# The order of work items in a segment, written anew for each of four places

## The chip, the cores and the metric

One core of a Trainium2 chip runs the whole kernel as one program. The metric is the device time of one execution in microseconds (us), here the median of three runs.

## The reference

Two branches are computed from the same input `x` (2048 tokens, width 640) and mixed by a gate:

```
g = sigmoid((x * gate_w).sum(-1))
b = (gelu(x @ w_gate) * (x @ w_up)) @ w_down
mem = mem0                                   # 8 rows
for s in range(64):                          # segments of 32 tokens
    h = concat(mem, x[32*s : 32*s+32])       # 40 rows
    q, k, v = h @ Wq, h @ Wk, h @ Wv         # 32 heads of 192
    p = softmax(mask(q @ k.T * 192**-0.5))
    o = (p @ v) @ Wo
    mem, a[s] = o[:8], o[8:]
out = g * a + (1 - g) * b
```

The recurrence is in `mem`: the first eight output rows of a segment are rows of the next segment's input. So the 64 segments run one after the other.

## The kernel before

The program first computes branch `b` and parks it in device memory. Then `segment(s)` runs 64 times. A segment at place `q = s % 4` works through a list of items, `PROGS[q]`. The list sets the order in which all engines' instructions are recorded; each engine then runs its own instructions in that order and waits on semaphores where it needs another engine's result.

The 32 heads are taken in four octets. Even segments go through the octets upward, odd ones downward. The items:

- `("g", n, k)`: step k of 5 of the projections of group n (`proj`). `GROUPS` says which: group 0 is Q and K of the first octet, group 1 V of the first and Q, K of the second, group 2 V of the second and Q, K of the third, group 3 V of the third and Q of the last, group 4 K of the last, group 5 V of the last. One projection step is four matmuls of 384 columns side by side (lines 1138 and 226), here called a quad. At place 0, V for the left-over rows is a further quad in groups 2, 3 and 5. After the fifth step ScalarE evacuates each result (line 1159 for Q and K, 1162 for V).
- `("tq", i)`, `("tk", i)`: VectorE transposes the rows of Q or K (line 1176). They issue nothing on TensorE.
- `("sc", i)`: the mask and the scores of octet i on TensorE (lines 1187 to 1202, 234), then maximum and subtraction on VectorE (1214, 1216).
- `("ex", i)`: the exponent on ScalarE (1226), sum, reciprocal and products on VectorE (1228 to 1233).
- `("pt", i)`: p transposed on TensorE (1249, 1254), evacuated by ScalarE (1267), for the last octet in part by VectorE.
- `("pv", i)`: p times V on TensorE (1282, 1284), evacuated by ScalarE (1310, 1320) and for the last octet also by VectorE (1314).
- `("wo", i, h)`: half of octet i's output projection (line 1338, for the last octet 1364, at place 3 line 1383).
- `("lf", u, x, k)`, `("le", ...)`: Q and K of the tokens that a later segment will need beside its memory rows ("left" work: line 930 and 226, evacuated by 1411 and 1413). Only items whose first number equals the place are run there. `("vb", k)` is V of that kind at place 3.

At a segment's end VectorE adds the halves of the output (1350, 1580), transposes the memory rows into the next segment's input (1583), and the next segment's group 0 starts.

The weights do not all fit on the chip. Thirteen pieces of Q, K and V and three of Wo are swapped in every segment: as soon as a piece of the first octet has been used, `swap_loads` has SyncE's queue load the piece of the last octet into its place (line 635). That one is used at the end of this segment and the beginning of the next. The queue of SyncE runs in the order of the list, too. Which pieces are resident follows from the order of the "g" and "wo" items in `seg_order`.

Before the change, places 0 and 2 share one list, `PROG`; place 1 has it with `("ex", 3)` moved just ahead of `("pv", 2)`; place 3 has its own, `PROG3`.

Of the kernel before, what the change touches and what calls it, by code (L numbers as in the profile page):

```python
# [238 lines left out]
def _build(nc, A_x, A_mem0, A_Wq, A_Wk, A_Wv, A_Wo, seg_len, w_gate, w_up, w_down,  # L239
# [282 lines left out]
    def piece_view(key, o):  # L522
        if key[0] == 3:
# [1 line left out]
        return bview(o, GQ)  # L525

    GROUPS = [[(0, 0), (1, 0)], [(2, 0), (0, 1), (1, 1)], [(2, 1), (0, 2), (1, 2)], [(2, 2), (0, 3)], [(1, 3)], [(2, 3)]]
    PROG = [("g", 0, 0), ("g", 0, 1), ("g", 0, 2), ("g", 0, 3), ("g", 0, 4), ("tq", 0), ("g", 1, 0), ("g", 1, 1),
# [12 lines left out]
    PROG3 = [("g", 0, 0), ("g", 0, 1), ("g", 0, 2), ("g", 0, 3), ("g", 0, 4), ("tq", 0), ("g", 1, 0), ("tk", 0),  # L541
# [8 lines left out]
    PROG1 = [item for item in PROG if item != ("ex", 3)]  # L550
    PROG1.insert(PROG1.index(("pv", 2)), ("ex", 3))
    PROGS = (PROG, PROG1, PROG, PROG3)
    assert NOCT == 4
    WOP = 4
    NWP = NT
# [14 lines left out]
    def seg_order(s):  # L570
        keys = []
        for item in PROGS[s % 4]:
            if item[0] == "g":
# [817 lines left out]
    mids, n_wos, to_store = set(), [], []  # L1391
    for x, prog in enumerate(PROGS):
        at = prog.index
# [5 lines left out]
        for u in range(2):  # L1399
# [6 lines left out]
            else:  # L1406
                assert at(("le", x, u, 0)) > max(at(("wo", 3, 1)), at(("pv", 3)))
    nqkvs = [[i for i, item in enumerate(prog) if item[0] == "g"][-1] for prog in PROGS]

# [36 lines left out]

    assert all(prog.index(("wo", NOCT - 2, 1)) < prog.index(("pv", NOCT - 1)) for prog in PROGS[:3])
    assert all(prog.index(("sc", NOCT - 1)) < prog.index(("pv", NOCT - 2)) and ("g", 3, EK) in prog[:prog.index(("sc", NOCT - 1))] for prog in PROGS)
    ek_at = [prog.index(("pv", NOCT - 2)) for prog in PROGS]

# [176 lines left out]
def bass_gated_mix__memory_aug_recurrent_mem_tr__glu_gated_geglu__prompt_kernel(  # L1627
    nc,
    A_x,
    A_mem0,  # L1630
    A_Wq,
    A_Wk,
    A_Wv,
    A_Wo,
    A_seg_len,
    B_x,
    B_w_gate,
    B_w_up,
    B_w_down,
    gate_w,  # L1640
    out,
):
    _build(nc, A_x, A_mem0, A_Wq, A_Wk, A_Wv, A_Wo, A_seg_len, B_w_gate, B_w_up, B_w_down, gate_w, out)
# [33 lines left out]
```

## Time and profile before

| | before |
|---|---|
| runs | 1657.43, 1655.54, 1647.93 us, median 1655.54 us |
| profiled execution, span | 2114.2 us (no other time is listed for it) |
| granted clock in the profiled execution | 0.654 |
| TensorE busy | 2098.0 us, 99% |
| VectorE, ScalarE, GpSimd busy | 48%, 38%, 26% |
| DMA | 499.28 MB, mean 236 GB/s over the span |

The profiled execution is one execution, and it took 459 us longer than the median of the timed runs. Shares of busy time are shares of its span. A matmul's end is modelled, so a busy TensorE need not be at its peak. TensorE's weight loads are listed as an engine of their own, PEld. In a row of a group, the numbers after the bar are the busy time in us, the mean of one in ns, and the engine's idle time just before, with what ended it. In a timeline row the first number is the start and the second the length, in us.

### The profile page before, as it was taken

Reading aid. Unit: us, or ns where it says so; the run is one execution under the profiler, and the core shown is the slowest. Engines: PE = TensorE matmul, PEld = TensorE weight load, DVE = VectorE, ACT = ScalarE, POOL = GpSimd, SP = SyncE. Lnnn points to the kernel's source line nnn. Section 1 sums busy time; section 2 is a strip of 40 time slices with the busy share of each in tenths; the row PEclk is TensorE's granted clock in tenths of the full one; section 3 lists DMA queues with packets and bytes.
Section 4 is the critical chain, followed back from the end, with each engine's and each line's share of the span. In section 5 each row is a group of like instructions: output and inputs, shape, how many; then the busy total and the mean of one; then the engine's idle time right before and its main releaser. Section 6 shows DMA issues by size and latency. Waiting matters only on the chain.

```text
span 2114.2 us, 75845 instructions
## 1 busy us (share of the span) xinstructions
PE 2098.0 (99%) x37107; PEld 958.1 (45%) x28147; DVE 1005.8 (48%) x3039; ACT 792.9 (38%) x1890; POOL 553.3 (26%) x1625
## 2 busy tenths in 40 slices
PE   9999999999999999999999999999999999999997
PEld 3444344444444444444444444444444444444444
DVE  4233254554545454545545454545455454545453
ACT  1111244343434343444434343434444343434342
POOL 1000023232232223232222323232322223222332
PEclk6666666666666666666666666666666666666666
DMA  9612577776768777677767677776777676777775
GB/s 319 182 33 57 184 268 260 248 270 232 253 219 275 244 258 241 227 255 254 274 233 249 221 268 249 255 251 225 248 256 270 239 258 212 261 256 249 254 264 174
DMA packets 275415, 499.28 MB, mean 236 GB/s; under 512 B 121119, under 2 KB 136327, under 8 KB 275079
## 3 DMA queue, kind: packets, MB, share of 16 engines
q1 hardware_dynamic: 271000, 491.30, 68.8%
q8 instruction: 255, 4.18, 0.8%
q10 hardware_dynamic: 4079, 3.14, 0.5%
q14 instruction: 81, 0.66, 0.1%
HBM read 473.25 MB, written 21.09 MB: 234 GB/s over the span
## 4 chain that ended last, share of the span: by engine, by line
PE 99%; DMA 0%; DVE 0%; SPq 0%; POOL 0%; ACT 0%; issue 0%; ACTq 0%; POOLq 0%; DVEq 0%
PE ps L226 26%; PE ps L1138 25%; PE ps L1338 9%; PE ps L1383 8%; PE ps L1282 4%; PE ps L930 4%; PE ps L839 4%; PE ps L836 4%; PE ps L862 3%; PE ps L1364 3%; PE ps L1187 2%; PE ps L1284 2%; PE ps L234 1%; PE ps L1195 1%; PE ps L971 1%; PE ps L1254 1%
## 5 line engine op out<-in xcount | busy, mean ns | idle before, releaser
L226 PE MATMUL ps<-arena 128*32 128x384 bf16 x8960 | 887.8, 430 | 0.4 <-ACT arena L1159 0.4
L1138 PE MATMUL ps<-arena 128*32 128x384 bf16 x8640 | 857.5, 420 | 2.0 <-DVE arena L1583 2.0
L1138 PEld LDWEIGHTS ps<-arena 128*32 128x32 bf16 x8640 | 303.3, 117 | 525.3 <-issue 379.7
L1176 DVE STREAM_TRANSPOSE arena<-arena 128x384 bf16<-128x384 bf16 x512 | 276.5, 562 | 144.1 <-ACT arena L1159 144.1
L1159 ACT ACTIVATE arena<-ps 128x384 bf16<-128x384 f32 x512 | 230.0, 491 | 160.1 <-PE ps L1138 160.1
L1214 DVE TENSOR_REDUCE arena<-ps 104x4 f32<-104x160 f32 x256 | 83.0, 324 | 340.2 <-PE ps L1202 340.2
L1338 PE MATMUL ps<-arena 128*32 128x320 bf16 x3456 | 241.0, 404 | 0.0
L1012 POOL COPY arena<-arena 128x96 bf16<-128x96 bf16 x256 | 70.2, 274 | 475.3 <-PE ps L1202 311.4
L1267 ACT ACTIVATE arena<-ps 128x448 bf16<-128x448 f32 x192 | 104.4, 544 | 237.7 <-PE ps L1254 233.3
L1179 POOL COPY arena<-arena 64x160 bf16<-64x160 bf16 x256 | 81.9, 320 | 385.5 <-DVE arena L1176 384.3
L1162 ACT ACTIVATE arena<-ps 128x384 bf16<-128x384 f32 x256 | 125.2, 489 | 128.1 <-PE ps L1138 127.5
L1383 PE MATMUL ps<-arena 128*64 128x320 bf16 x1536 | 169.6, 387 | 0.0
L1226 ACT ACTIVATE ps<-ps 104x160 f32<-104x160 f32 x256 | 74.8, 292 | 239.5 <-DVE ps L1216 239.5
L1320 ACT ACTIVATE arena<-ps 128x480 bf16<-128x480 f32 x192 | 109.5, 570 | 93.8 <-PE ps L1284 85.7
L930 PE MATMUL ps<-arena 128*32 128x384 bf16 x1280 | 142.5, 408 | 0.0
L1338 PEld LDWEIGHTS ps<-arena 128*32 128x32 bf16 x3456 | 113.3, 129 | 56.9 <-ACT arena L1261 18.1
L1282 PE MATMUL ps<-arena 128*64 128x160 bf16 x1536 | 135.2, 263 | 0.0
L1284 PE MATMUL ps<-arena 128*64 128x64 bf16 x1536 | 128.6, 225 | 0.0
L1228 DVE TENSOR_REDUCE arena<-ps 104x4 f32<-104x160 f32 x256 | 81.8, 319 | 88.4 <-ACT ps L1226 87.4
L1383 PEld LDWEIGHTS ps<-arena 128*64 128x64 bf16 x1536 | 93.2, 127 | 49.4 <-issue 9.6
L1282 PEld LDWEIGHTS ps<-arena 128*64 128x64 bf16 x1536 | 94.1, 126 | 42.8 <-ACT arena L1159 23.0
L1411 ACT ACTIVATE arena<-ps 128x384 bf16<-128x384 f32 x120 | 57.3, 491 | 123.9 <-DVE arena L1580 74.0
(102 smaller groups left out, 2518.2 us busy)
## 6 DMA issues: line engine op xcount, KB each, us to landing
arena<-in_A_Wk_dram SPq DMA_DIRECT2D x335, 384.0 KB, 5.8
arena<-in_A_Wv_dram SPq DMA_DIRECT2D x335, 384.0 KB, 8.4
arena<-in_A_Wo_dram SPq DMA_DIRECT2D x205, 480.0 KB, 4.3
arena<-in_A_Wq_dram SPq DMA_DIRECT2D x209, 384.0 KB, 4.8
arena<-left_qk_scratch SPq DMA_DIRECT2D x126, 96.0 KB, 3.9
left_qk_scratch<-arena SPq DMA_DIRECT2D x49, 192.0 KB, 4.6
left_qk_scratch<-arena SPq DMA_DIRECT2D x30, 96.0 KB, 3.7
ffn_b_scratch<-arena ACTq DMA_DIRECT2D x16, 160.0 KB, 2.3
```

The costliest lines, as they stand in the source:

```text
L226: return e.add_instruction(mybir.InstMatmult(name=nm, start_tensor_calc=like["start"], stop_tensor_calc=stop, tile_size=(128, 32), tile_po ...
L930: fns.append(lambda e, outp=outp, rhs=rhs, j=j: e.matmul(outp, lhs, rhs, start=(k == 0), stop=(k == KT - 1), tile_position=(0, 32 * j)))
L1138: fns.append(lambda e, outp=outp, rhs=rhs, j=j: e.matmul(outp, lhs, rhs, start=(k == 0), stop=(k == KT - 1), tile_position=(0, 32 * j)))
L1159: S_.add("act", lambda e, m=m, bk=bk: e.activation(out=rows_sb[m], in_=ps[:, bk, 0:384], func=ACTF.Copy), reads=[r_ps[bk]], writes=[r_rows ...
L1162: S_.add("act", lambda e, i=i, bk=bk: e.activation(out=v_sb[i % NVB].rearrange("p (c n) -> p c n", c=3), in_=ps[:, bk, 0:384].rearrange("p ...
L1176: S_.add("dve", lambda e: e.transpose(out=dst[:, :, 0:L], in_=rows_sb[m].rearrange("p (c r) -> p c r", r=L)), reads=[r_rows[m]], writes=[r ...
L1267: S_.add("act", lambda e: e.activation(out=PT, in_=ps[:, bank, 0:PTW + 128], func=ACTF.Copy), reads=[r_ps[bank]], writes=[r_PT], name="pT ...
L1282: return [lambda e: e.matmul(full, v[:, e0:e0 + 64], PTm[:, i], start=True, stop=False, tile_position=(0, 64 * i), skip_group_check=True), ...
L1284: lambda e: e.matmul(part, vl[:, e0:e0 + 64], PTl[:, i], start=False, stop=True, tile_position=(0, 64 * i), skip_group_check=True)]
L1320: S_.add("act", lambda e: e.activation(out=apx(u[:, 0, 0, :], [[rs, na], [3 * rs, 4], [1, R]]), in_=ps[:, A, 0:na * W].rearrange("p (c t r ...
L1338: fns.append(lambda e, i=i, t=t, j=j, gv=gv: e.matmul(ps[32 * j:32 * j + 32, bank, 0:2 * DJ].rearrange("p (h n) -> p h n", h=2), lhs2[i], ...
L1383: S_.add("pe", [lambda e, i=i, g_=g_, c=c, p=p, u=u: e.matmul(ps[64 * i:64 * i + 64, LB, 0:2 * DJ], u[:, c, :], g_[:, c, 2 * DJ * i:2 * DJ ...
```

## The change

The lists of items are replaced. Each place has its own list now, with the items that run there alone; the left-over items of other places, which were skipped, no longer stand in it. Each place's list holds the same items as before, in another order. In the words of its author, all work items of a segment were searched anew for each of the four places separately, with a replay that uses the durations of the trace. `GROUPS` and all functions stay as they are.

```diff
--- before.py
+++ after.py
@@ -525,31 +525,45 @@
         return bview(o, GQ)
 
     GROUPS = [[(0, 0), (1, 0)], [(2, 0), (0, 1), (1, 1)], [(2, 1), (0, 2), (1, 2)], [(2, 2), (0, 3)], [(1, 3)], [(2, 3)]]
-    PROG = [("g", 0, 0), ("g", 0, 1), ("g", 0, 2), ("g", 0, 3), ("g", 0, 4), ("tq", 0), ("g", 1, 0), ("g", 1, 1),
-            ("tk", 0), ("g", 1, 2), ("sc", 0), ("g", 1, 3), ("ex", 0), ("g", 1, 4), ("g", 2, 0), ("g", 2, 1),
-            ("g", 2, 2), ("lf", 1, 0, 0), ("pt", 0), ("tq", 1), ("tk", 1), ("sc", 1), ("g", 2, 3), ("g", 2, 4),
-            ("tq", 2), ("ex", 1), ("lf", 2, 1, 0), ("lf", 1, 0, 1), ("lf", 1, 0, 2), ("pv", 0), ("g", 3, 0),
-            ("tk", 2), ("g", 3, 1), ("g", 3, 2), ("g", 3, 3), ("pt", 1), ("lf", 2, 1, 1), ("g", 3, 4), ("sc", 2),
-            ("ex", 2), ("pv", 1), ("wo", 0, 0), ("g", 4, 0), ("g", 4, 1), ("lf", 0, 1, 0), ("g", 4, 2),
-            ("lf", 1, 0, 3), ("lf", 1, 0, 4), ("lf", 1, 1, 0), ("lf", 1, 1, 1), ("le", 1, 0, 0), ("tq", 3),
-            ("g", 4, 3), ("le", 1, 0, 1), ("g", 4, 4), ("g", 5, 0), ("g", 5, 1), ("pt", 2), ("wo", 0, 1), ("tk", 3),
-            ("sc", 3), ("pv", 2), ("g", 5, 2), ("wo", 1, 0), ("ex", 3), ("g", 5, 3), ("wo", 1, 1), ("g", 5, 4),
-            ("wo", 2, 0), ("pt", 3), ("wo", 2, 1), ("pv", 3), ("lf", 1, 1, 2), ("lf", 2, 1, 2), ("lf", 0, 1, 1),
-            ("lf", 0, 1, 2), ("wo", 3, 0), ("wo", 3, 1), ("lf", 2, 1, 3), ("lf", 2, 1, 4), ("le", 2, 1, 0),
-            ("le", 2, 1, 1), ("lf", 1, 1, 3), ("lf", 1, 1, 4), ("le", 1, 1, 0), ("le", 1, 1, 1), ("lf", 0, 1, 3),
-            ("lf", 0, 1, 4), ("le", 0, 1, 0), ("le", 0, 1, 1)]
+    PROG0 = [("g", 0, 0), ("g", 0, 1), ("g", 0, 2), ("g", 0, 3), ("g", 0, 4), ("tq", 0), ("g", 1, 0), ("g", 1, 1),
+             ("g", 1, 2), ("g", 1, 3), ("tk", 0), ("g", 1, 4), ("sc", 0), ("g", 2, 0), ("g", 2, 1), ("tq", 1),
+             ("ex", 0), ("tk", 1), ("g", 2, 2), ("g", 2, 3), ("g", 2, 4), ("pt", 0), ("sc", 1), ("tk", 2),
+             ("tq", 2), ("ex", 1), ("g", 3, 0), ("g", 3, 1), ("g", 3, 2), ("pv", 0), ("g", 3, 3), ("g", 3, 4),
+             ("pt", 1), ("sc", 2), ("g", 4, 0), ("g", 4, 1), ("tq", 3), ("g", 4, 2), ("g", 4, 3), ("ex", 2),
+             ("g", 4, 4), ("tk", 3), ("pv", 1), ("g", 5, 0), ("wo", 0, 0), ("g", 5, 1), ("pt", 2), ("wo", 0, 1),
+             ("sc", 3), ("ex", 3), ("pv", 2), ("wo", 1, 0), ("g", 5, 2), ("g", 5, 3), ("wo", 1, 1), ("g", 5, 4),
+             ("wo", 2, 0), ("pt", 3), ("lf", 0, 1, 0), ("wo", 2, 1), ("pv", 3), ("lf", 0, 1, 1), ("lf", 0, 1, 2),
+             ("wo", 3, 0), ("wo", 3, 1), ("lf", 0, 1, 3), ("lf", 0, 1, 4), ("le", 0, 1, 0), ("le", 0, 1, 1)]
+    PROG1 = [("g", 0, 0), ("g", 0, 1), ("g", 0, 2), ("g", 0, 3), ("g", 0, 4), ("tq", 0), ("tk", 0), ("g", 1, 0),
+             ("g", 1, 1), ("g", 1, 2), ("sc", 0), ("g", 1, 3), ("ex", 0), ("g", 1, 4), ("g", 2, 0), ("g", 2, 1),
+             ("g", 2, 2), ("pt", 0), ("tq", 1), ("g", 2, 3), ("tk", 1), ("g", 2, 4), ("sc", 1), ("pv", 0),
+             ("tq", 2), ("g", 3, 0), ("g", 3, 1), ("lf", 1, 0, 0), ("g", 3, 2), ("ex", 1), ("g", 3, 3),
+             ("lf", 1, 0, 1), ("g", 3, 4), ("tk", 2), ("lf", 1, 0, 2), ("pt", 1), ("sc", 2), ("tq", 3), ("ex", 2),
+             ("g", 4, 0), ("g", 4, 1), ("lf", 1, 0, 3), ("pv", 1), ("g", 4, 2), ("lf", 1, 0, 4), ("le", 1, 0, 0),
+             ("le", 1, 0, 1), ("g", 4, 3), ("g", 4, 4), ("g", 5, 0), ("wo", 0, 0), ("pt", 2), ("lf", 1, 1, 0),
+             ("wo", 0, 1), ("lf", 1, 1, 1), ("g", 5, 1), ("tk", 3), ("sc", 3), ("pv", 2), ("wo", 1, 0),
+             ("wo", 1, 1), ("g", 5, 2), ("g", 5, 3), ("wo", 2, 0), ("ex", 3), ("g", 5, 4), ("lf", 1, 1, 2),
+             ("pt", 3), ("wo", 2, 1), ("pv", 3), ("wo", 3, 0), ("wo", 3, 1), ("lf", 1, 1, 3), ("lf", 1, 1, 4),
+             ("le", 1, 1, 0), ("le", 1, 1, 1)]
+    PROG2 = [("g", 0, 0), ("g", 0, 1), ("g", 0, 2), ("g", 0, 3), ("g", 0, 4), ("tk", 0), ("g", 1, 0), ("g", 1, 1),
+             ("tq", 0), ("g", 1, 2), ("g", 1, 3), ("g", 1, 4), ("sc", 0), ("g", 2, 0), ("g", 2, 1), ("tk", 1),
+             ("tq", 1), ("g", 2, 2), ("g", 2, 3), ("ex", 0), ("g", 2, 4), ("sc", 1), ("lf", 2, 1, 0), ("pt", 0),
+             ("tq", 2), ("g", 3, 0), ("tk", 2), ("ex", 1), ("g", 3, 1), ("g", 3, 2), ("pv", 0), ("g", 3, 3),
+             ("g", 3, 4), ("sc", 2), ("tq", 3), ("pt", 1), ("ex", 2), ("g", 4, 0), ("g", 4, 1), ("g", 4, 2),
+             ("g", 4, 3), ("g", 4, 4), ("pv", 1), ("wo", 0, 0), ("wo", 0, 1), ("g", 5, 0), ("pt", 2), ("tk", 3),
+             ("sc", 3), ("wo", 1, 0), ("ex", 3), ("pv", 2), ("g", 5, 1), ("lf", 2, 1, 1), ("g", 5, 2), ("g", 5, 3),
+             ("wo", 1, 1), ("g", 5, 4), ("wo", 2, 0), ("pt", 3), ("wo", 2, 1), ("pv", 3), ("lf", 2, 1, 2),
+             ("lf", 2, 1, 3), ("wo", 3, 0), ("wo", 3, 1), ("lf", 2, 1, 4), ("le", 2, 1, 0), ("le", 2, 1, 1)]
     PROG3 = [("g", 0, 0), ("g", 0, 1), ("g", 0, 2), ("g", 0, 3), ("g", 0, 4), ("tq", 0), ("g", 1, 0), ("tk", 0),
-            ("g", 1, 1), ("g", 1, 2), ("g", 1, 3), ("sc", 0), ("ex", 0), ("g", 1, 4), ("g", 2, 0), ("g", 2, 1),
-            ("g", 2, 2), ("g", 2, 3), ("pt", 0), ("tq", 1), ("tk", 1), ("g", 2, 4), ("g", 3, 0), ("sc", 1),
-            ("pv", 0), ("g", 3, 1), ("tq", 2), ("tk", 2), ("g", 3, 2), ("g", 3, 3), ("ex", 1), ("g", 3, 4),
-            ("sc", 2), ("g", 4, 0), ("g", 4, 1), ("g", 4, 2), ("g", 4, 3), ("pt", 1), ("tq", 3), ("wo", 0, 0),
-            ("ex", 2), ("g", 4, 4), ("wo", 0, 1), ("tk", 3), ("pv", 1), ("g", 5, 0), ("pt", 2), ("sc", 3),
-            ("wo", 1, 0), ("ex", 3), ("wo", 1, 1), ("pv", 2), ("g", 5, 1), ("g", 5, 2), ("g", 5, 3), ("pt", 3),
-            ("g", 5, 4), ("wo", 2, 0), ("pv", 3), ("wo", 2, 1), ("wo", 3, 0), ("wo", 3, 1), ("vb", 0), ("vb", 1),
-            ("vb", 2), ("vb", 3), ("vb", 4)]
-    PROG1 = [item for item in PROG if item != ("ex", 3)]
-    PROG1.insert(PROG1.index(("pv", 2)), ("ex", 3))
-    PROGS = (PROG, PROG1, PROG, PROG3)
+             ("g", 1, 1), ("g", 1, 2), ("sc", 0), ("g", 1, 3), ("ex", 0), ("g", 1, 4), ("g", 2, 0), ("tq", 1),
+             ("g", 2, 1), ("g", 2, 2), ("g", 2, 3), ("pt", 0), ("tk", 1), ("g", 2, 4), ("sc", 1), ("g", 3, 0),
+             ("g", 3, 1), ("tk", 2), ("tq", 2), ("ex", 1), ("pv", 0), ("g", 3, 2), ("g", 3, 3), ("g", 3, 4),
+             ("g", 4, 0), ("g", 4, 1), ("g", 4, 2), ("g", 4, 3), ("sc", 2), ("g", 4, 4), ("pt", 1), ("wo", 0, 0),
+             ("tq", 3), ("tk", 3), ("wo", 0, 1), ("ex", 2), ("pv", 1), ("sc", 3), ("g", 5, 0), ("pt", 2),
+             ("ex", 3), ("wo", 1, 0), ("wo", 1, 1), ("pv", 2), ("g", 5, 1), ("g", 5, 2), ("pt", 3), ("g", 5, 3),
+             ("g", 5, 4), ("wo", 2, 0), ("pv", 3), ("wo", 2, 1), ("wo", 3, 0), ("wo", 3, 1), ("vb", 0), ("vb", 1),
+             ("vb", 2), ("vb", 3), ("vb", 4)]
+    PROGS = (PROG0, PROG1, PROG2, PROG3)
     assert NOCT == 4
     WOP = 4
     NWP = NT
```

## The prediction

> **What bounds it now.** The page comes first, for the span, the busy engines and the clock.
>
> ```profile
> span 2114.2 us, 75845 instructions
> PE 2098.0 (99%) x37107; PEld 958.1 (45%) x28147; DVE 1005.8 (48%) x3039; ACT 792.9 (38%) x1890; POOL 553.3 (26%) x1625
> q1 hardware_dynamic: 271000, 491.30, 68.8%
> ```
>
> ```profile
> core 0: 2114.2 us, clock 0.654
> ```
>
> TensorE is busy for 2098.0 of 2114.2 us at a mean granted clock of 0.654. No other engine passes 48%; the DMA queue is at 68.8%. This is an execution at a lowered clock: the three timed runs have a median of 1655.5 us, 459 us less. The 2098.0 us are 2098.0 x 0.654 = 1372 us of work at full clock; with the 16 us outside TensorE that is 1388 us. So 1655.5 us fits two readings, and the page cannot choose between them: TensorE always busy at a clock of 1372/1639 = 0.84, or a full clock with 268 us in which TensorE waits. What a new order is worth hangs on that, so I cost it at several clocks.
>
> [...]
>
> Next, the windows of segments 40 to 43, one round over the four places, and one row of the chain of waits for the price of a projection step.
>
> ```profile
> sum 116.00, PE 116.00 PEld 53.87 DVE 57.82 ACT 47.06 POOL 33.57; mean PE 29.00 PEld 13.47 DVE 14.45 ACT 11.76 POOL 8.39
> ```
>
> ```profile
> 273.42 1.71 PE ps L1138 x28
> ```
>
> A round takes 116.00 us and TensorE is busy in all of it; there are 16 rounds. Four matmuls of 384 columns run side by side; such a quad takes 1.71/7 = 0.244 us here, 0.160 at full clock.
>
> **What the change moves.** It adds and removes nothing: each place has the same items, so the same instructions and the same bytes. GROUPS and the order of the weight pieces stay as they are, so the resident set and the swapped pieces stay too. The price of the edit is therefore entirely in the cover: the TensorE work that lies in program order between an item and the one that waits for its result on another engine. I count it from the lists, at full clock: a "g" step is 0.16 times its quads (2, 3, 3, 2, 1, 1 for groups 0 to 5, one more at place 0 in groups 2, 3, 5), "lf" 0.32, a "wo" half 960 columns or 0.40 (0.80 at place 3). For "sc", "pt", "pv", the starts of TensorE's timeline:
>
> ```profile
> 375.14 0.25 PE L1187 MATMUL ps<-arena 128*40 128x160 bf16 x2
> 375.52 0.35 PE L1138 MATMUL ps<-arena 128*32 128x384 bf16 x4
> ...
> 379.81 0.28 PE L1249 MATMUL ps<-arena 104*32 104x80 bf16 x4
> 380.07 0.25 PE L1187 MATMUL ps<-arena 128*40 128x160 bf16 x2
> ...
> 382.45 0.26 PE L1282 MATMUL ps<-arena 128*64 128x160 bf16 x2
> 382.95 0.35 PE L1138 MATMUL ps<-arena 128*32 128x384 bf16 x4
> ```
>
> From a first to the next item's first: 0.38, 0.26 and 0.50 us, times 0.654 = 0.25, 0.17, 0.33 at full clock. The latency that each cover must hide comes from the other engines' groups, whose means do not depend on TensorE's clock:
>
> ```profile
> L1176 DVE STREAM_TRANSPOSE arena<-arena 128x384 bf16<-128x384 bf16 x512 | 276.5, 562 | 144.1 <-ACT arena L1159 144.1
> L1159 ACT ACTIVATE arena<-ps 128x384 bf16<-128x384 f32 x512 | 230.0, 491 | 160.1 <-PE ps L1138 160.1
> L1162 ACT ACTIVATE arena<-ps 128x384 bf16<-128x384 f32 x256 | 125.2, 489 | 128.1 <-PE ps L1138 127.5
> L1267 ACT ACTIVATE arena<-ps 128x448 bf16<-128x448 f32 x192 | 104.4, 544 | 237.7 <-PE ps L1254 233.3
> L1216 DVE TENSOR_TENSOR ps<-ps,arena 104x160 f32<-104x160 f32 x256 | 85.1, 333 | 8.8
> L1214 DVE TENSOR_REDUCE arena<-ps 104x4 f32<-104x160 f32 x256 | 83.0, 324 | 340.2 <-PE ps L1202 340.2
> L1228 DVE TENSOR_REDUCE arena<-ps 104x4 f32<-104x160 f32 x256 | 81.8, 319 | 88.4 <-ACT ps L1226 87.4
> L1226 ACT ACTIVATE ps<-ps 104x160 f32<-104x160 f32 x256 | 74.8, 292 | 239.5 <-DVE ps L1216 239.5
> L1232 DVE TENSOR_TENSOR arena<-ps,arena 104x128 bf16<-104x128 f32 x256 | 74.6, 292 | 8.8
> L1233 DVE TENSOR_TENSOR arena<-ps,arena 104x32 bf16<-104x32 f32 x256 | 46.3, 181 | 0.0
> L1230 DVE RECIPROCAL arena<-arena 104x4 f32<-104x4 f32 x256 | 45.6, 178 | 8.8
> ```
>
> And the end of segment 40, in the timeline:
>
> ```profile
> 1441.29 0.35 PE L930 MATMUL ps<-arena 128*32 128x384 bf16 x4
> ...
> 1441.93 1.38 PEld L1364 LDWEIGHTS ps<-arena 128*32 128x32 bf16 x48 [0.36 <-DVE arena L1314]
> ...
> 1443.40 0.40 PE L930 MATMUL ps<-arena 128*32 128x384 bf16 x4
> ...
> 1443.70 0.25 DVE L1580 TENSOR_TENSOR arena<-ps,arena 128x64 bf16<-128x64 f32 x1 [1.21 <-PE ps L1364]
> ...
> 1443.98 0.26 DVE L1583 STREAM_TRANSPOSE arena<-arena 128x64 bf16<-128x64 bf16 x1
> ...
> 1444.34 0.48 PE L1138 MATMUL ps<-arena 128*32 128x384 bf16 x4
> ```
>
> Now term by term, in us of a round at full clock, places 0 to 3, before then after; a hand-over counts as about 0.05 (between L1583's end at 1444.24 and the matmul lie 0.10).
>
> Last keys to "sc 3": one evacuation and one transposition, 0.49 + 0.56 + 0.10 = 1.15. Cover 1.21, 0.89, 0.89, 1.46; then 1.94, 1.93, 1.46, 2.10. Short by 0.52; then by 0.
>
> Group 0 to "sc 0": two evacuations, 1.64. Cover 1.44, 1.44, 1.44, 1.92; then 2.40, 1.44, 2.40, 1.44. Short by 0.60; then 0.40.
>
> Group 1 to "sc 1": three evacuations, 2.13. Cover 2.09, 1.93, 1.61, 2.89; then 3.62, 2.57, 2.65, 2.57. Short by 0.76; then 0.
>
> "sc" to "pt": the seven softmax rows sum to 1.92, with hand-overs 2.1. Before it lacks 0.25 ("pt 2" at place 2, cover 1.85) and twice 0.09 ("pt 3" at places 1 and 2, 2.01), 0.43 together; then the smallest cover is 2.17, short by 0.
>
> "pt" to "pv": 0.54 with hand-overs 0.60. Before, "pv 3" has 0.40 at three places and "pv 1" 0.57 at place 1: short by 0.63; then 0.40 is left at places 1 and 2: 0.40.
>
> "pv 3" to "wo 3": 1441.29 to 1441.93, 0.64. Cover 0.64, 0.32, 0.32, 0.80; then 0.64, 0.00, 0.64, 0.80. Short by 0.64 both times: place 2 gains what place 1 loses.
>
> "wo 3" to the next segment: 1443.40 to 1444.34, 0.94. Cover 0.64, 0.64, 0.64, 0.80; then place 2 has one "lf" left, 0.32. Short by 1.04; then 1.36.
>
> Sum: 4.62 before, 2.80 after, 1.82 a round, 29 us in 16 rounds.
>
> Then what the queues do in order. Before, "ex 1" at places 0 to 2 is issued behind the three evacuations of group 2, which follow "sc 1": from "sc 1" the exponent starts 1.47 after "g 2 4", so p is ready after 4.1, 3.8 and 3.8 us, against covers of 3.53, 3.21, 2.89: 2.0 short. After, "g 2 4" stands ahead of "sc 1"; p needs 3.2, 2.55, 3.1 against 2.73, 2.89, 2.67: 0.9 short. That gains 1.1 a round. It has a price: at places 0 and 2 "pt 0" now follows "g 2 4" too, so its evacuation queues behind those three and is ready 1.47 + 0.60 = 2.07 after "g 2 4", where "pv 0" comes at 1.86 and 1.70: 0.21 and 0.37 lost, 0.58. Net 0.52, 8 us.
>
> Together 37 us at full clock. These waits lie one behind the other in one stream, and a wait early in a segment lengthens every later cover, so they do not add: bounds are 0 and 37 us, and I take the middle, 18 us. At a clock of 0.84 every cover is 1.2 times as long; the same terms give 1.75 before and 1.78 after, nothing. At 0.654, 1.53 times: before only "wo 3" lacks 0.15 at two places, 0.30 a round; after, place 1 lacks 0.64 and the end of place 2 0.45, 1.09. There the change costs 0.79 x 16 = 13 us, so a profile again at 0.65 should span about 2127 us. The waits fit: at 0.654 the two ends of a segment are what TensorE's weight loads wait for on VectorE.
>
> ```profile
> PEld ps L1138 <- DVE arena L1583: 34.0, 77, 1.0
> PEld ps L1364 <- DVE arena L1314: 16.5, 45, 0.4
> ```
>
> **The rivals.** First, no difference: the timed clock is near 0.84 and TensorE has no wait to lose. For it: the profile's 99%. Against: 0.84 is not the clock of this trace. It gives 1655.5 us within 5.
>
> Second, slower by the swapped keys. Half of the weights are swapped in each segment, and group 4 needs the last of five key pieces. The queue of SyncE, segment 41, whose first matmul is that at 1444.34, and the landing time of such a load:
>
> ```profile
> 1447.65 2.35 SPq L635 DMA_DIRECT2D arena<-in_A_Wk_dram  x3
> ```
>
> ```profile
> arena<-in_A_Wk_dram SPq DMA_DIRECT2D x335, 384.0 KB, 5.8
> ```
>
> The last is issued by 1450.00 and lands at 1455.8, 11.5 us into the segment; at full clock group 0 is consumed 0.8 us sooner, so 10.7. "g 4 4" has 12.7, 13.0, 11.4, 10.9 us of TensorE work ahead of it before, and 11.7, 12.0, 10.4, 9.9 after: the change needs the piece 1 us earlier everywhere. With 10.7 it is short by 0.3 and 0.8 at places 2 and 3, 1.1 a round, 18 us; with 11.5 it adds 2.0 a round, 32 us. It decides if less than 1 us of waiting lies ahead of group 4. That gives 1673 us. For it: transfers scarcely get faster with the clock. Against: waits in front (group 0 and 1, "pt 0") push group 4 back.
>
> Third, slower by the ends of segments: if the covers inside a segment already suffice and only the ends count, the 0.79 of the low clock applies, 1668 us.
>
> That the change does nothing can be left out: the order on TensorE differs nearly everywhere.
>
> **How the numbers follow.** The forecast has 0.45, and 1655.5 - 18 = 1637 us. No difference has 0.17, the keys 0.25, the ends 0.13. About 0.5% (8 us) is what a measurement of this kernel can tell from no change. Faster: the forecast and 0.02 of the first rival, 0.47. Same: 0.13 of the first and 0.02 of the third, 0.15. Slower: 0.25, 0.11 and 0.02, 0.38. The range goes from the whole 37 us and some 7 us for the runs' own spread, 1612 us, to between the two prices of the keys, 1682 us. The forecast's own range is 1612 to 1647.
>
> **What would show it.** In a profile at 0.65: about 2127 us, more wait of L1364's weight loads on L1314 and of L1138's on L1583. In a profile at a higher clock: weight loads that wait on DMAs of the keys would show the second rival; waits on L1176 and L1233 gone, with "pv 0" waiting on L1267, the forecast. A timed median above 1647 us makes the forecast wrong.

## The result and the profile after

The changed kernel takes 1696.89 us (median of four runs, 1688.43 to 1700.65), the kernel before 1651.74 us (four runs, 1645.56 to 1657.43). The ratio is 1.0273 [1.0225, 1.0321]: slower by 45 us, and outside the range that was predicted.

The profile of before that the prediction quotes fell in an execution at a granted clock of 0.654; every run whose clock is recorded besides, and every profile below, has a mean clock of 0.98 to 0.998. So the profile after is set beside a second profile of the unchanged kernel, the first of the experiments below (1651.42 us, ratio 1.0005 [0.9985, 1.0026]). Its page and its cores:

```profile
span 1650.2 us, 75845 instructions
PE 1564.8 (95%) x37107; PEld 774.4 (47%) x28147; DVE 997.8 (60%) x3039; ACT 784.6 (48%) x1890; POOL 549.6 (33%) x1625
q1 hardware_dynamic: 271000, 491.30, 85.1%
PE 68%; DMA 12%; DVE 7%; SPq 4%; ACT 4%; issue 3%; POOL 1%; DVEq 0%; ACTq 0%; POOLq 0%
```

```profile
core 0: 1650.2 us, clock 0.996
```

The same of the kernel after (its time is 1693.53 us):

```profile
span 1691.8 us, 76086 instructions
PE 1555.9 (92%) x37107; PEld 775.0 (46%) x28147; DVE 985.0 (58%) x3039; ACT 780.1 (46%) x1890; POOL 549.0 (32%) x1625
q1 hardware_dynamic: 271000, 491.30, 83.5%
PE 62%; DMA 28%; SPq 4%; DVE 3%; issue 2%; ACT 1%; POOL 0%; DVEq 0%; ACTq 0%; POOLq 0%
```

```profile
core 0: 1691.8 us, clock 0.988
```

Matmuls and megabytes are equal. TensorE is busy for 9 us less, and sits idle for 1691.8 - 1555.9 = 136 us where it sat idle for 85. On the chain of work that ended last, VectorE's share falls from 7% to 3%, as the prediction would have it; that of the DMAs rises from 12% to 28%. What TensorE's weight loads and matmuls wait for names them (us in total, times, longest). First before:

```profile
PEld ps L1138 <- DVE arena L1583: 48.4, 123, 0.9
PEld ps L1249 <- DVE arena L1233: 33.0, 75, 1.0
PEld ps L1364 <- DMA arena<-in_A_Wo_dram: 10.2, 17, 1.0
PEld ps L1138 <- DMA arena<-in_A_Wk_dram: 4.2, 9, 0.9
PE ps L1364 <- DMA arena<-in_A_Wo_dram: 6.7, 14, 0.8
PE ps L1138 <- DMA arena<-in_A_Wk_dram: 1.6, 3, 0.6
```

And after, where the lines of the functions stand 14 lower (1378 is 1364 before, 1247 is 1233, 1281 is 1267):

```profile
PEld ps L1152 <- DVE arena L1597: 48.5, 110, 0.9
PEld ps L1378 <- DMA arena<-in_A_Wo_dram: 46.7, 42, 3.4
PEld ps L1152 <- DMA arena<-in_A_Wk_dram: 25.9, 41, 1.7
PEld ps L1296 <- ACT arena L1281: 16.1, 45, 0.5
PEld ps L1263 <- DVE arena L1247: 8.8, 23, 0.9
PE ps L1378 <- DMA arena<-in_A_Wo_dram: 38.2, 41, 3.2
PE ps L1152 <- DMA arena<-in_A_Wk_dram: 15.9, 32, 1.3
```

The wait of "pt" on the softmax has gone from 33.0 to 8.8, and "pv" now waits on line 1267: both signs that were named for the forecast. But the matmuls of "wo 3" wait 38.2 us for swapped pieces of Wo, 31.5 more than before, and the projections wait 15.9 us for keys, 14.3 more. Sorted by segments, 28.2 of the 38.2 us lie at place 1, where before has 0.8; of the 15.9 us, 5.3 lie at place 2 and 10.2 at place 3.

Where the wait for Wo comes from shows in segment 41, at place 1. SyncE's queue before (start, length, line, transfer, count); the segment's first matmul starts at 1116.76, the next segment's at 1139.66:

```profile
1129.34 0.90 SPq L635 DMA_DIRECT2D arena<-in_A_Wo_dram  x2
1131.45 0.59 SPq L1419 DMA_DIRECT2D left_qk_scratch<-arena  x1
1132.28 0.44 SPq L635 DMA_DIRECT2D arena<-in_A_Wo_dram  x1
```

And after, from 1136.66 to 1160.81:

```profile
1150.70 0.59 SPq L1433 DMA_DIRECT2D left_qk_scratch<-arena  x1
1151.34 2.06 SPq L649 DMA_DIRECT2D arena<-in_A_Wo_dram  x3
```

Before, the first two pieces of Wo are asked for 12.6 us into the segment. After, all three are asked for at 14.7 to 16.7 us, behind a store of left-over queries (96 KB) that before stood ahead of the third piece alone. The same two segments in windows of 4 us from their first matmul (stretch; length; busy time of the engines; granted clock, DMA share, GB/s), before:

```profile
1120.76:1124.76 4.00, 4.00 (x118) 1.43 (x58) 2.92 (x10) 1.99 (x5) 1.18 (x5) 1.00 1.02 389
...
1128.76:1132.76 4.00, 3.87 (x96) 1.95 (x78) 3.11 (x9) 2.83 (x7) 0.85 (x3) 1.00 1.05 386
1132.76:1136.76 4.00, 3.37 (x96) 2.11 (x96) 1.88 (x8) 1.69 (x4) 2.39 (x5) 1.00 1.02 322
1136.76:1139.66 2.90, 2.79 (x88) 1.66 (x74) 1.58 (x7) 1.11 (x4) 1.14 (x3) 1.00 0.70 212
```

And after:

```profile
1140.66:1144.66 4.00, 4.00 (x126) 1.42 (x66) 2.49 (x9) 2.90 (x8) 0.82 (x4) 1.00 1.02 388
...
1148.66:1152.66 4.00, 4.00 (x125) 2.52 (x117) 3.04 (x9) 2.48 (x7) 1.41 (x3) 1.00 0.90 313
1152.66:1156.66 4.00, 3.41 (x96) 2.14 (x88) 2.05 (x9) 2.44 (x7) 1.57 (x4) 1.00 0.90 273
1156.66:1160.81 4.15, 1.97 (x64) 0.89 (x49) 1.06 (x5) 0.14 (x2) 1.14 (x3) 0.99 0.78 258
```

In this profile the swaps of a segment are one nearly unbroken row of transfers: before the change, the DMA share is over 1.0 in every window from 4 to 20 us into the segment. After it, the share is 0.90 in both windows from 12 to 20 us: the row has a hole, since the pieces of Wo, asked for late and behind the store, do not join on to those of V. The hole is not made up here: the segment is 24.15 us long instead of 22.90, and TensorE pays in the last window (1.97 of 4.15 us busy). The rows of "wo 3" there:

```profile
1158.56 0.45 PE L1378 MATMUL ps<-arena 128*32 128x160 bf16 x13 [1.42 <-DMA arena<-in_A_Wo_dram]
1159.77 0.39 PE L1378 MATMUL ps<-arena 128*32 128x160 bf16 x12 [0.76 <-DMA arena<-in_A_Wo_dram]
```

Before, in the same segment, 46 of its 48 matmuls run in one stretch:

```profile
1137.81 1.01 PE L1364 MATMUL ps<-arena 128*32 128x160 bf16 x46
```

A second effect goes with the wait. From 1160.7 to 1164.1 us TensorE's granted clock is 0.50, and the next segment's first matmuls last 0.51 us, where they last 0.35 before. The profile after has nine such stretches of 3.4 us, eight of them within a few us of the end of a segment at place 1; before has none until its last 20 us. At half the clock, nine stretches take at most about 15 us of TensorE's time (an estimate, 9 x 3.4 x 0.5); how much of that shows in the loss no run separates. A table below has their number in other runs.

### The profile page after: what moved, and what is told of

Same layout as the page of the kernel before. It is cut to its first block, busy times and chain, and to the rows that moved or that the text cites. A ratio compares the mean times of both kernels' runs of the same rounds, so it can differ in the third digit from the quotient of the medians.

```text
span 1691.8 us, 76086 instructions
## 1 busy us (share of the span) xinstructions
PE 1555.9 (92%) x37107; PEld 775.0 (46%) x28147; DVE 985.0 (58%) x3039; ACT 780.1 (46%) x1890; POOL 549.0 (32%) x1625
## 3 DMA queue, kind: packets, MB, share of 16 engines
q8 instruction: 255, 4.18, 1.0%
## 4 chain that ended last, share of the span: by engine, by line
PE 62%; DMA 28%; SPq 4%; DVE 3%; issue 2%; ACT 1%; POOL 0%; DVEq 0%; ACTq 0%; POOLq 0%
PE ps L1152 18%; PE ps L226 16%; DMA arena<-in_A_Wo_dram 13%; DMA arena<-in_A_Wk_dram 11%; PE ps L1397 7%; PE ps L1352 4%; DMA arena<-in_A_Wv_dram 4%; PE ps L1296 3%; PE ps L944 2%; PE ps L1201 2%; PE ps L1378 2%; SPq L649 2%; PE ps L853 2%; PE ps L850 2%; PE ps L876 1%
## 5 line engine op out<-in xcount | busy, mean ns | idle before, releaser
L1152 PE MATMUL ps<-arena 128*32 128x384 bf16 x8640 | 653.9, 331 | 35.2 <-DMA arena<-in_A_Wk_dram 15.9
L226 PE MATMUL ps<-arena 128*32 128x384 bf16 x8960 | 642.2, 329 | 0.4 <-ACT arena L1173 0.2
L1152 PEld LDWEIGHTS ps<-arena 128*32 128x32 bf16 x8640 | 227.6, 97 | 417.6 <-issue 270.6
L1176 ACT ACTIVATE arena<-ps 128x384 bf16<-128x384 f32 x256 | 125.2, 489 | 183.2 <-PE ps L1152 181.0
L1352 PE MATMUL ps<-arena 128*32 128x320 bf16 x3456 | 179.7, 302 | 13.4 <-issue 8.9
L1026 POOL COPY arena<-arena 128x96 bf16<-128x96 bf16 x256 | 69.3, 271 | 273.4 <-PE ps L1216 190.3
L1296 PE MATMUL ps<-arena 128*64 128x160 bf16 x1536 | 117.8, 241 | 2.9 <-issue 2.9
L1397 PE MATMUL ps<-arena 128*64 128x320 bf16 x1536 | 118.4, 303 | 1.0 <-issue 0.3
L1352 PEld LDWEIGHTS ps<-arena 128*32 128x32 bf16 x3456 | 91.1, 96 | 59.3 <-ACT arena L1275 15.1
L944 PE MATMUL ps<-arena 128*32 128x384 bf16 x1280 | 113.1, 334 | 5.6 <-issue 5.5
L1378 PE MATMUL ps<-arena 128*32 128x160 bf16 x2304 | 61.1, 236 | 55.9 <-DMA arena<-in_A_Wo_dram 38.2
L1342 POOL COPY arena<-arena 128x96 bf16<-128x96 bf16 x192 | 51.3, 267 | 180.3 <-ACT arena L1324 99.7
L1298 PE MATMUL ps<-arena 128*64 128x64 bf16 x1536 | 103.1, 193 | 2.4 <-issue 2.4
```

Source lines behind the costliest of these rows:

```text
L226: return e.add_instruction(mybir.InstMatmult(name=nm, start_tensor_calc=like["start"], stop_tensor_calc=stop, tile_size=(128, 32), tile_po ...
L944: fns.append(lambda e, outp=outp, rhs=rhs, j=j: e.matmul(outp, lhs, rhs, start=(k == 0), stop=(k == KT - 1), tile_position=(0, 32 * j)))
L1152: fns.append(lambda e, outp=outp, rhs=rhs, j=j: e.matmul(outp, lhs, rhs, start=(k == 0), stop=(k == KT - 1), tile_position=(0, 32 * j)))
L1176: S_.add("act", lambda e, i=i, bk=bk: e.activation(out=v_sb[i % NVB].rearrange("p (c n) -> p c n", c=3), in_=ps[:, bk, 0:384].rearrange("p ...
L1296: return [lambda e: e.matmul(full, v[:, e0:e0 + 64], PTm[:, i], start=True, stop=False, tile_position=(0, 64 * i), skip_group_check=True), ...
L1298: lambda e: e.matmul(part, vl[:, e0:e0 + 64], PTl[:, i], start=False, stop=True, tile_position=(0, 64 * i), skip_group_check=True)]
```

## The experiments

Three theories: W, the pieces of Wo are released and queued too late, at place 1 above all; K, the swapped keys are late for group 4 (the prediction's second rival); E, the ends of the segments (its third). In the expectations of the first seven runs W is not parted from K yet: there K means all swapped pieces, those of Wo too. Ratios are to the unchanged kernel, run beside each on the same chip; gains and losses in us are differences of ratios times 1651 us.

**Before, again.** The unchanged kernel, for a profile at the clock of the timed runs.

> The kernel before, unchanged, for a profile at the clock of the timed runs. Theory K (weights swapped in late: with the changed order TensorE waits for the landing of key, value and output weight pieces): a time of 1650 +- 8 us, clock about 0.98, and the same lines of weight loads that wait on DMA as in the changed kernel, but for clearly less time: under 60 us against the 28% of the chain (some 470 us, most of it transfer time that other work runs beside) there. Theory E (ends of segments: the evacuation of the last octet and the last additions): DMA waits about as long as in the changed kernel, and the waits of L1364 on L1314 and of L1138 on L1583 shorter by some 40 us.

It is the profile of before used above. Its clock is 0.996, not 0.84, and TensorE idles for 85 us, not for the 268 us of the prediction's second reading. Busy time did not shrink in step with the clock: 2098.0 us at 0.654 would be 1378 us at 0.996, and 1564.8 us are listed.

**Smaller swaps, old lists and new.** The same edit in both kernels, in `load_piece`: of each swapped piece of Q, K and V half is loaded, of each swapped piece of Wo a third.

```diff
-        S_.add("sp", lambda e: e.dma_start(piece_view(key, res_off[key]), piece_src(key)), writes=[r_res[key]],
+        w, x = piece_view(key, res_off[key]), piece_src(key)
+        if name.startswith("swap"):
+            w, x = (w[:, 0:1], x[:, 0:1]) if key[0] == 3 else (w[:, 0:GQ // 4], x[:, 0:GQ // 4])
+        S_.add("sp", lambda e: e.dma_start(w, x), writes=[r_res[key]],
```

> The order of before, but each swapped piece of Q, K and V brings only half of its columns and each swapped piece of Wo a third, so the results are not the reference's. Theory K: a gain over before, 1590 to 1640 us, since before already waits for some pieces. Theory E: within 10 us of before, 1650.

> The changed order with the same small swaps. Theory K: the 45 us are gone, this is as fast as the order of before with small swaps or faster, by the 18 to 37 us that the covers promised. Theory E: it stays 40 us slower than the order of before with small swaps.

With small swaps the old lists take 1597.20 us, 0.9678 [0.9655, 0.9700], and the new lists 1553.14 us, 0.9409 [0.9391, 0.9427]. The new order is then 44 us faster than the old one; with full swaps it is 45 us slower. From the pages, old lists first, then new:

```profile
PE 1548.1 (97%) x37107; PEld 774.1 (49%) x28147; DVE 995.7 (62%) x3039; ACT 784.6 (49%) x1890; POOL 549.7 (34%) x1625
q1 hardware_dynamic: 271000, 266.38, 56.0%
```

```profile
PE 1511.3 (97%) x37107; PEld 767.9 (49%) x28147; DVE 977.9 (63%) x3039; ACT 779.1 (50%) x1890; POOL 549.6 (35%) x1625
q1 hardware_dynamic: 271000, 266.38, 57.5%
```

At the same number of matmuls, 37 us show as less busy time of TensorE (a matmul's end is modelled, so short waits can count as busy), and few as less idle time. The wait of "pt" on the softmax falls from 38.3 to 9.6 us, and weight loads wait 2.5 us in all for swapped pieces with the new lists, not at all with the old. So the covers do what they were meant to do, and the whole loss, with the gain that it swallows, hangs on the size of the swaps. Even the old order pays 53 us for them.

**One place at a time.** The old lists with the new list at one place only (AFTER0 to AFTER3 are the new lists):

```diff
-    PROGS = (PROG, PROG1, PROG, PROG3)
+    PROGS = (AFTER0, PROG1, PROG, PROG3)    # only place 0
+    PROGS = (PROG, AFTER1, PROG, PROG3)     # only place 1
+    PROGS = (PROG, PROG1, AFTER2, PROG3)    # only place 2
+    PROGS = (PROG, PROG1, PROG, AFTER3)     # only place 3
```

> The new list at place 0 alone, the other places as before. Theory K, first octet's output projection 1.2 us later and last keys 1 us earlier: some 10 to 15 us slower than before, 1660 to 1667. Theory E (the ends of places 1 and 2 only): no slower, 1645 to 1652.

> The new list at place 1 alone. Theory K: the output projection of the first octet starts 1.6 us later, keys 1 us earlier: 10 to 15 us slower, 1660 to 1667. Theory E: nothing left between pv 3 and wo 3, 0.32 us x 16 = 5 us slower and up to 10, 1655 to 1662.

> The new list at place 2 alone. Theory K: last keys 1 us earlier with the least work ahead of them: 10 to 15 us slower, 1660 to 1667. Theory E: 0.32 us less at the end but 0.32 more before it: within 5 us of before.

> The new list at place 3 alone. Theory K: last keys 1 us earlier and needed after 9.9 us of work, the earliest of all: 10 to 18 us slower, 1660 to 1670. Theory E: its end is as before, so within 5 us of before.

| new list at | us | ratio |
|---|---|---|
| place 0 | 1657.49 | 1.0026 [1.0004, 1.0048] |
| place 1 | 1689.00 | 1.0230 [1.0204, 1.0255] |
| place 2 | 1650.84 | 1.0004 [0.9984, 1.0025] |
| place 3 | 1654.12 | 1.0026 [1.0007, 1.0045] |

The four excesses sum to 0.0286, the whole change has 0.0273: the places add, and place 1 has 38 of the 45 us. No expectation had 1689 us there. The last keys alone (K) would put the loss at places 2 and 3. The keys are late there: with place 2 alone, in the view of waits,

```profile
PEld ps L1147 <- DMA arena<-in_A_Wk_dram: 19.8, 33, 1.0
```

where before has 4.2 us. Yet that kernel is no slower. With place 3 alone the same row has 13.2 us, and 4 us are lost, where 10 to 18 were expected. With place 1 alone it is Wo that is late:

```profile
PEld ps L1375 <- DMA arena<-in_A_Wo_dram: 38.9, 36, 3.5
```

**Place 1, Wo released earlier.** The kernel with the new list at place 1 only, and in it one item moved up, so that its piece of Wo is used, and its place free, sooner:

```diff
-... ("pv", 1), ("g", 4, 2), ... ("g", 5, 0), ("wo", 0, 0), ("pt", 2), ...
+... ("pv", 1), ("wo", 0, 0), ("g", 4, 2), ... ("g", 5, 0), ("pt", 2), ...
```

> The new list at place 1 alone, as in the run that was 38 us slower, but with the first half of the first octet's output projection moved up behind pv 1, as in the kernel before. Theory W (the swapped pieces of Wo are released and queued too late, so the transfers pause and the last octet's projection waits): back to 1648 to 1656. Theory K (the last keys 1 us earlier): stays above 1680. Theory E (nothing between pv 3 and wo 3): stays 5 to 10 us slower than before.

1655.84 us, 1.0044 [1.0028, 1.0060]: one item takes back 31 of the 38 us. The wait goes from 38.9 us to

```profile
PEld ps L1375 <- DMA arena<-in_A_Wo_dram: 11.9, 19, 1.1
```

The last items of the segment are untouched, so E is not the cause of these 31 us. But the 7 us that stay are what E expected (5 to 10), and its wait is there: the matmuls of "wo 3" wait for the evacuations of "pv 3" (lines 1310 and 1314 of before)

```profile
PE ps L1375 <- ACT arena L1321: 5.4, 11, 0.5
PE ps L1375 <- DVE arena L1325: 3.1, 7, 0.5
```

where before has 0.5 and 0.9 us. These 7.1 us more all lie at place 1.

**Place 1, the store behind the loads.** The same kernel with the new list at place 1, the item left late, and the store of left-over queries kept back with that of the keys, which is queued behind the loads of Wo:

```diff
-            (mid_store if m == 0 else mid_later.append)((g, o, m, dst, rd))
+            mid_later.append((g, o, m, dst, rd))
```

> The new list at place 1 alone, first projection late as there, but the store of the left-over queries (96 KB in small packets), which that list puts ahead of the Wo loads in SyncE's queue, is queued behind them. If the store ahead of them is the cause: 1650 to 1660. If it is the late release itself: 1680 or more. If both share: about 1668.

1670.17 us, 1.0129 [1.0109, 1.0150]: 17 of the 38 us come back with the store alone; the release of the place stays late. The waits of "wo 3" fall to nearly the same as with the item moved up:

```profile
PEld ps L1375 <- DMA arena<-in_A_Wo_dram: 14.0, 24, 1.3
```

though 14 us more of the time are left, so these waits alone are not the whole price. Where the 14 us sit was not settled.

**The other way round.** The kernel before, with this one item put late at place 1:

```diff
+    PROG1.remove(("wo", 0, 0))
+    PROG1.insert(PROG1.index(("g", 5, 0)) + 1, ("wo", 0, 0))
```

> The lists of before, with one item moved at place 1: the first half of the first octet's output projection goes down behind the first step of group 5, where the new list has it; the store then stands ahead of the Wo loads too. Theory W: about as slow as the new list at place 1, 1680 to 1692. Theories K and E, whose items are not touched: within 8 us of 1650.

1679.24 us, 1.0190 [1.0160, 1.0221], 31 us slower by one item, with the wait that the new list has:

```profile
PEld ps L1366 <- DMA arena<-in_A_Wo_dram: 32.3, 33, 2.5
```

The issues and landings in the traces show the late row directly. The table has the third piece of Wo at place 1, in us from the segment's first matmul (medians of 16 segments), and the number of stretches at a granted clock of 0.50 that begin ahead of the last 20 us of the span:

| lists | asked for | landed | stretches at 0.50 |
|---|---|---|---|
| before | 15.5 | 21.1 | 0 |
| new list at place 1 | 16.5 | 23.6 | 11 |
| the same, Wo early | 15.1 | 21.2 | 2 |
| the same, store behind the loads | 15.1 | 21.4 | 3 |
| before, Wo late | 16.7 | 22.9 | 8 |
| all new lists | 16.5 | 23.0 | 9 |

**All new lists, Wo early at place 1.** The move of one item at place 1, as above, in the changed kernel.

> All four new lists, with that one item at place 1 moved up behind pv 1. Theory W: the 38 us go, 1650 to 1662; if the covers inside the segment then pay as they did with small swaps, down to 1640. Theory K: 1690.

1669.87 us, 1.0116 [1.0082, 1.0151]: 26 of the 45 us come back, fewer than the 38 that W expected, and 19 are left. Its waits:

```profile
PEld ps L1152 <- DMA arena<-in_A_Wk_dram: 28.3, 48, 1.4
PEld ps L1378 <- DMA arena<-in_A_Wo_dram: 22.8, 29, 1.9
PEld ps L1152 <- DMA arena<-in_A_Wv_dram: 10.5, 26, 0.8
```

**And the keys later.** On top of that, the last two steps of group 4 put behind "wo 0 0" at places 2 and 3, by the waits above the test of K:

```diff
-... ("g", 4, 3), ("g", 4, 4), ("pv", 1), ("wo", 0, 0), ...                      # place 2
+... ("pv", 1), ("wo", 0, 0), ("g", 4, 3), ("g", 4, 4), ...
-... ("g", 4, 3), ("sc", 2), ("g", 4, 4), ("pt", 1), ("wo", 0, 0), ...           # place 3
+... ("sc", 2), ("pt", 1), ("wo", 0, 0), ("g", 4, 3), ("g", 4, 4), ...
```

> All four new lists with the projection moved up at place 1, as in the run that was 21 us slower than before, and besides the last two steps of group 4 (the last keys) put down behind the first half of the first octet's output projection at places 2 and 3, some 0.7 and 1.2 us later. Theory K for what is left (the keys land too late for the earlier group 4): most of the 21 us go, 1650 to 1658, and the waits on transfers of Wk fall from 28 us to under 10. Rival (what is left lies in the Wo pieces at places 0 and 2): 1665 to 1675, with the Wo waits as they were.

1663.88 us, 1.0074 [1.0048, 1.0100]. The waits for keys are gone, 28.3 to 3.4 us, but the time falls by 7 us only, and the intervals overlap:

```profile
PEld ps L1136 <- DMA arena<-in_A_Wv_dram: 16.0, 38, 1.1
PEld ps L1362 <- DMA arena<-in_A_Wo_dram: 12.8, 22, 1.1
PEld ps L1136 <- DMA arena<-in_A_Wk_dram: 3.4, 6, 1.2
```

Waits for V have grown in their place, from 10.5 to 16.0. The edit also lets "wo 0 0" run sooner at both places, and the waits for Wo fell from 22.8 to 12.8 us; so the 7 us are not the keys' alone. K is a real wait, but at best a small part of the loss.

**The old order, fed better.** If a piece of Wo still comes late in the kernel before, the old lists should gain by a second half of the output projection done sooner and the store behind the loads:

```diff
-            ("g", 4, 4), ("g", 5, 0), ("g", 5, 1), ("pt", 2), ("wo", 0, 1), ("tk", 3),
+            ("g", 4, 4), ("wo", 0, 1), ("pt", 2), ("g", 5, 0), ("g", 5, 1), ("tk", 3),
...
-            (mid_store if m == 0 else mid_later.append)((g, o, m, dst, rd))
+            mid_later.append((g, o, m, dst, rd))
```

> The lists of before with the second half of the first octet's output projection moved up ahead of pt 2 at places 0 to 2, so that the third Wo piece is queued about 1.2 us sooner, and with the store of the left-over queries queued behind the Wo pieces. Theory W, if the third piece still comes late in the kernel before: 5 to 15 us faster than before, 1635 to 1645. If the transfers are one unbroken row by then (it lands 21 us into the segment in all orders but the late ones): no change, 1646 to 1654.

A miss: 1665.76 us, 1.0082 [1.0051, 1.0113]. The wait of weight loads for Wo falls little, from 10.2 to 8.6 us, and the kernel is slower. The trace says where: a segment at place 0 takes 24.49 us on average instead of 23.45, and the other places change by -0.2 to 0.1 us. The store is issued at place 1 alone, so the items moved up ("wo 0 1" and "pt 2") are the likely cost. The third piece of Wo is asked for 1.5 us sooner at place 0 and lands 0.2 us sooner, and TensorE's waits for nothing that the profile shows grow there from 14.1 to 23.7 us. No version here with full swaps beats the kernel before.

## Why the prediction was wrong

**The step that failed** stands at the head of the part on the change: bytes and order of the pieces stay, so "the price of the edit is therefore entirely in the cover", and the cover was counted to other engines only. But an item that uses a swapped piece also frees its place, and the work from there to the user of the next piece is the cover of a transfer. By the prediction's own prices, from the start of "wo 0 0" to "wo 3" at place 1, this is 6.85 us before: ten steps of groups 4 and 5 (1.60), five "lf" (1.60), six halves of Wo (2.40), "sc", two "pt", two "pv" (1.25). After, four steps and three "lf" are left of them: 0.64 + 0.96 + 2.40 + 1.25 = 5.25 us. These 1.6 us, 26 us in 16 rounds, could have been a rival. The one item moved cost 31 us in the old list, and gave back 31 in the new one; the third piece of Wo then lands 1.8 us later and 2.4 us sooner. The count alone does not price every place: at place 0 this cover falls by 1.12 us, from 7.01 to 5.89, and only 4 us in all were lost there, so it matters how much is left. That the store comes ahead of the loads, worth 17 us, was to be seen in the lists too.

**Why the row of transfers was not looked at.** The prediction looked at the landing of the keys, not at the row as a whole. It named the queue's 68.8% beside a TensorE at 99%, and in the next lines scaled TensorE to full clock, but not the queue. Transfers hardly get shorter with the clock: 0.688 x 2114.2 = 1455 us of them in 1655 us would be 88%. The profile at a clock of 0.996 has 85.1%, or 1404 us. That half of the weights are swapped in a segment is not so either: it is 13 of 60 pieces of Q, K and V and 3 of 16 of Wo. No term was worked out from that sentence.

**The covers** were right in direction and too small: 44 us with small swaps, where the bounds were 0 and 37 and 18 was taken. The row of "pt" waiting on line 1233 loses 24 us from before to after. Two premises of the count hold: in the second profile of before, at a clock of 1.00, the first six quads of segment 41 begin 0.164 us apart (from 1116.76 to 1117.58 us), where 0.160 was worked out for full clock; and the other engines' means hardly depend on the clock of TensorE (L1176 562 ns at 0.654 and 558 at 0.996, L1159 491 and 493, L1267 544 and 543). The end of the segment, line 1583, was to cost 0.32 us more a round, 5 us; the weight loads that wait for it have 48.4 and 48.5 us. What went wrong is not the direction of this term: with full swaps its gain does not show, and the runs fit that it exists only where the row of transfers ends earlier.

**The rivals.** No difference at a clock of 0.84: the clock is 0.996 before and 0.988 after. So the reading with a full clock was the nearer one. What lowered the clock to 0.654 in the first profile no run shows. The swapped keys: the mechanism and the place were right (waits at places 2 and 3, 14.3 us more of TensorE in all, for 18 predicted), the share in the time was not: 0.0004 with place 2 alone, 7 us when the waits were taken away. The keys gave the range its upper end, 1682 us; that it lies only 15 us under the result is luck. The ends of the segments: not the cause of the 31 us at place 1 that came back while the ends stayed as they were, but of the size of the 7 us that were left there. The prediction netted this term to nothing, since place 2 was to gain what place 1 loses; the matmuls of "wo 3" waited about 7 us more for "pv 3" at place 1, and at place 2 there were only 0.4 us of such waits to gain.

**What stays open.** With Wo early and the keys late, 12 us of loss remain, of which the end of place 1 may account for about 7 (the waits of "wo 3" for "pv 3" are there again, 8.6 us against 1.4), and the 44 us of the covers are missing besides. That waits move from one piece to the next (keys down from 28.3 to 3.4 us, V up from 10.5 to 16.0) fits a row of transfers that sets the end whatever waits for it, but no run changes the row's length alone at full size. Nor was it settled why the old order, fed sooner, loses 14 us at place 0.

## What to carry to other kernels

Count a change of order twice: once for who waits for the result, once for who waits for the place that it frees, and take the DMA queue along when a profile at a low clock is scaled to a higher one (its share was 68.8% at 0.654 and 85.1% at 0.996). Where swapped weights fill a queue nearly all the time, as here, a hole in that row can be lost for good, as the one at place 1 was (segment 41 took 24.15 us instead of 22.90), so try first the order in which an item that releases a load comes before one that only fills a cover (31 us here), and no small store goes ahead of large loads (17 us here, a store of 96 KB ahead of loads of 480 KB). That sooner is not always better the last experiment shows (14 us slower). A search over orders by replay needs the transfers, with their queue and their length, among its resources; whether the replay of this edit had them, no run here tells.

## What was not expected of the hardware

TensorE's waits for nothing that the profile shows ("issue") go with the traffic here. The groups of the same matmuls, the output projection of the first three octets, in before and in before with small swaps (behind the last bar the idle time, and what ended it):

```profile
L1338 PE MATMUL ps<-arena 128*32 128x320 bf16 x3456 | 183.2, 300 | 10.8 <-issue 6.3 <-DMA arena<-in_A_Wo_dram 1.0
```

```profile
L1341 PE MATMUL ps<-arena 128*32 128x320 bf16 x3456 | 181.2, 300 | 2.9 <-issue 0.6
```

6.3 us against 0.6; after has 8.9. Over all of TensorE's matmuls such waits sum to 19 to 39 us in every profile with full swaps at a clock of 0.98 or more, and to 0.6 and 0.2 us in the two with small swaps. The page also lists 4.18 MB of instructions among the DMA queues (1.0% of the engines' time, before and after); whether these transfers have to do with the waits, no run shows.

In three of the windows of 4 us above, the DMA engines move 386 to 389 GB/s at a share of 1.02 to 1.05, with one core at work. The mean over the span is 303 GB/s before and 295 after.
